# Two FNet and two MLP layers in fp32: a layer-norm shift on ScalarE, high parts first at the start, and weight steps moved in the first MLP half

## The chip, the cores and the metric

The kernel runs on 1 core of one Trainium2 chip. A core has a matrix engine (TensorE, "PE" in the profile, its weight loads "PEld"), VectorE (DVE), ScalarE (ACT), GpSimd (POOL) and SyncE (SP), which here only issues transfers. Each engine runs its own instructions in the order in which they were written; between engines they wait on semaphores. SBUF is the on-chip memory, PSUM the eight banks that matmuls write. The metric is device time in microseconds, the median of several runs.

## The reference, cut to what matters

```python
def _A_ref(x, dft_seq_re, dft_seq_im, dft_hid_re, dft_hid_im):
    a = jnp.einsum("bsd,ed->bse", x, dft_hid_re)
    b = jnp.einsum("bsd,ed->bse", x, dft_hid_im)
    return jnp.einsum("ts,bse->bte", dft_seq_re, a) - jnp.einsum("ts,bse->bte", dft_seq_im, b)

def _B_ref(x, w1, b1, w2, b2):
    y = _layernorm(x, axis=-1)
    h = _gelu(jnp.einsum("bsd,df->bsf", y, w1) + b1)
    return jnp.einsum("bsf,fd->bsd", h, w2) + b2

x = x + _A_ref(_layernorm(x), ...)     # twice this pair,
x = x + _B_ref(_layernorm(x), ...)     # with the same weights
```

x is 1 x 2048 x 576, the MLP's inner width is 4608, all in fp32. _B_ref normalises its input once more, so the kernel takes both norms in one.

## The kernel before, in words

Every matrix product is split for precision: each operand is stored as a high part (a copy in fp32r) and a low part (the operand minus the high part), and a product is three matmul passes, high x high, high x low, low x high (PASSES: which part of the left operand u, of the right operand w). ScalarE makes high parts, VectorE low parts. Most products are also cut by Strassen's scheme into seven block products per 2 x 2 blocks, numbered 1 to 7, with sums of blocks as operands.

A layer has three stages.

- Sequence transform (class Sequence). The rows of x come in eight pairs p of 128-row tiles. A pair is loaded, its mean and variance are taken (norm_stats: BN_STATS, BN_AGGR), it is normalised, and split: high_left and low_left for the block of DFT coefficients (1024 columns), high_z and low_z for the data (three blocks of 288, then one more), right_sums, high_sums and low_sums for Strassen's sums. fill() is a generator that writes these steps; run() advances it and writes first_mms(p), 48 matmuls of 288 columns for the first two output tiles, which fill all eight PSUM banks. After the eighth pair come the other 14 output tiles (mms, post), whose coefficients stream in.
- Hidden transform (function hidden), for half of the rows at a time, eight tiles n. After each tile's 54 matmuls VectorE adds the residual, and norms(n) takes the statistics, makes the normalised tile, and later PE transposes it (turn_blocks). stats() gives, in the small tile mv: mean, variance, power -1/2 of the variance, and the shift = -mean x power. normalize() is one ScalarE activation with that scale and shift. The tile n = 7 is "plain": it is normalised by VectorE and needs no shift.
- MLP (function mlp), for the same half. inner(q) makes 2 x 128 inner features: seven products in the order ORDER, each with an add on VectorE, then gelu on ScalarE. outer(g, i, side) multiplies them by w2, one Strassen product i in two product halves (jj), each 12 matmuls of 288 columns into one of two bank pairs, after which VectorE adds the bank pair into its goal (576 columns). A bank pair comes round again two product halves later. Per group g there is inner, a row of outer with four products (eight halves), inner, and a row with three products (six halves); OUTER names the products.

Only in the first MLP half of layer 1 are the weights themselves split and stored for the three later halves. weights() is a background generator for w1; pump() takes its next step, alternately VectorE's low part (384 columns) with ScalarE's next high part, and the store. make(g) does it for w2 (low parts of 2 x 288 columns on VectorE). What sets their place is written by hand: at[0] counts positions in a group, 0 to 6 the seven products of the first inner, 7 to 14 the eight halves, 15 to 21 the second inner, 22 to 27 the six halves. BEHIND lists the positions after which pump() is called; make(g) returns steps with their positions. The activation work of an inner (tasks, eight steps: gelu and high parts on ScalarE, low parts and Strassen's sums on VectorE, later ones on POOL) is taken by work(n) behind outer's halves and the next inner's products. slot[0] counts the halves of a row.

In the last group of the last half (ends), POOL adds the buffer uv, which holds product 6, to products 3, 7 and 4 before rows are stored.

Of the kernel before, what the change touches and what calls it, by code (L numbers as in the profile page):

```python
# [10 lines left out]
AF = mybir.ActivationFunctionType  # L11
# [147 lines left out]
def spectral_mixer(ctx: ExitStack, tc: tile.TileContext, x, dh, c0, cs, w1, b1, w2, b2, out):  # L159
# [58 lines left out]
    def stats(src, twice=False, plain=False):  # L218


        st, mv = (v[:, 0] for v in moments())
        st = st.rearrange("p (a b) -> p a b", a=2)
        for h in range(2):
            nc.vector.bn_stats(st[:, h, :], src[:, h, :])
        nc.vector.bn_aggr(mv[:, 0:2], st.rearrange("p a b -> p (a b)"))
        if twice:
            nc.vector.tensor_scalar(mv[:, 2:3], mv[:, 1:2], 1 + EPS, EPS * EPS, op0=OP.mult, op1=OP.add)  # L227
        else:
            nc.vector.tensor_scalar(mv[:, 2:3], mv[:, 1:2], EPS, None, op0=OP.add)
        nc.gpsimd.tensor_tensor(mv[:, 3:4], mv[:, 2:3], power[:, 0:1], op=OP.pow)  # L230
        if plain:
            return mv
        nc.gpsimd.tensor_tensor(mv[:, 4:5], mv[:, 0:1], mv[:, 3:4], op=OP.mult)
        nc.gpsimd.tensor_tensor(mv[:, 4:5], power[:, 2:3], mv[:, 4:5], op=OP.subtract)  # L234
        return mv

    def stats_of_pair(src, plain, later):

        st, mv = moments()
        for h in range(4):  # L240
            nc.vector.bn_stats(st[:, h // 2, h % 2 * 6:h % 2 * 6 + 6], src[:, h, :])
        for h in range(2):
            nc.vector.bn_aggr(mv[:, h, 0:2], st[:, h])
        (nc.gpsimd if later else nc.vector).tensor_scalar(mv[:, :, 2], mv[:, :, 1], EPS, None, op0=OP.add)
        nc.gpsimd.tensor_tensor(mv[:, :, 3], mv[:, :, 2], power[:, 0:2], op=OP.pow)
        if plain:
            return mv
        nc.gpsimd.tensor_tensor(mv[:, :, 4], mv[:, :, 0], mv[:, :, 3], op=OP.mult)
        nc.gpsimd.tensor_tensor(mv[:, :, 4], power[:, 2:4], mv[:, :, 4], op=OP.subtract)
        return mv  # L250

    def normalize(dst, src, mv):
# [72 lines left out]
    class Sequence:  # L325
        def __init__(self, src, early):

            self.src, self.early = src, early
            self.Z, self.parts, self.b12, self.v, self.x, self.mv = [None] * NP, {}, {}, {}, {}, {}
            self.ready, self.closed, self.wish = 0, False, list(range(NP))  # L330
            self.normal, self.xs, self.before = set(), [], self.prepare()
            self.pieces = self.fill()


# [31 lines left out]
        def fill(self):  # L366
# [49 lines left out]
            for p in range(NP):  # L416
# [11 lines left out]
                if p == 1 and self.early:  # L428
# [94 lines left out]
        def load_left(self, p):  # L523
            for t in range(PLAIN):
                dma(self.lv[p][:, 4 * t:4 * t + 4], c0[p][:, t])

        def norm_stats(self, p):
            if p not in self.mv:
                self.mv[p] = stats_of_pair(self.x[p], p == 0 and not self.early, p > 2)

        def normalize(self, p):
            for h in range(2):
                at = slice(2 * h, 2 * h + 2)
                if p == 0 and not self.early:
                    v, mv = self.x[p][:, at], self.mv[p][:, h]
                    nc.vector.tensor_scalar(v, v, mv[:, 0:1], mv[:, 3:4], op0=OP.subtract, op1=OP.mult)
                    continue
                normalize(self.x[p][:, at], self.x[p][:, at], self.mv[p][:, h])

        def high_left(self, p):  # L540
# [48 lines left out]
        def first_mms(self, p):  # L589
            c, z, b = self.left(p), self.Z[p](7, 2, DH), self.b12[p](2, DH)  # L590
            right = {(1, 1): z[:, 0], (2, 2): z[:, 1], (2, 1): z[:, 2], (1, 2): b}
            for t in range(PLAIN):
                for i in (1, 2):
                    for j in (1, 2):
                        o = banks[4 * (1 - t) + 2 * (i - 1) + j - 1][:, :DH]
                        for k in (1, 2):
                            for n, (u, w) in enumerate(PASSES):
                                mm(o, c[:, u, 4 * t + 2 * (i - 1) + k - 1], right[k, j][:, w],
                                   p == 0 and k == 1 and n == 0, p == NP - 1 and k == 2 and n == 2)
            self.own.give(self.parts.pop(p))  # L600
            clock[0] += 1

# [277 lines left out]
    def hidden(h, mlp):  # L880
# [18 lines left out]
        def norms(n):  # L899

            if n % 2 == 0:
                t8[n // 2] = t8s.take()
            v = t8[n // 2](8, DH)
            tile_x = xv[:, :, order[n]]

            z = v[:, 2:4] if n % 2 == 0 else v[:, 0:2]
            mv = stats(tile_x, twice=True, plain=n == NP - 1)
            yield
            if n < NP - 1:
                normalize(z, tile_x, mv)  # L910
# [160 lines left out]
    def mlp(hid, store, first, ends, before, after):  # L1071
# [40 lines left out]
        def make(g):  # L1112
# [157 lines left out]
        def outer(g, i, side):  # L1270
            for jj in range(2):
# [183 lines left out]
```

## Time and profile before

| | |
|---|---|
| median of 3 runs | 2653.71 us (2652.15 to 2653.80) |
| profiled execution | 2650.84 us |
| its span | 2649.0 us |
| TensorE clock granted | 1.00 |
| TensorE busy | 2623.9 us |
| VectorE, ScalarE, GpSimd busy | 1833.9, 1107.5, 823.3 us |

The span runs from the first to the last instruction of the profile; 1.84 us of the execution lie around it. A row of a timeline is: start, length, engine, line, operation, what it writes and reads, sizes, count, and in brackets the idle time before it and what ended it. Line L209 is mm(), L196 and L199 are add() and sub() for all engines, so rows are told apart by tiles and sizes: A and R are the two SBUF heaps (R holds split parts), bank is PSUM, moments the small tile.

The main stages in the profile: the first pairs from 8.6 to 62.5 us, the rest of the sequence transform to about 380, the hidden transform to 443, the first MLP half to 862; then hidden and MLP for the other rows, and from about 1336 the second layer.

### The profile page before, as it was taken

How to read it: one execution, taken by the hardware profiler on the slowest of the kernel's cores; microseconds unless marked ns; L12 is line 12 of the kernel's file. 1: busy time of each engine (PE TensorE's matmuls, PEld its weight loads, DVE VectorE, ACT ScalarE, POOL GpSimd, SP SyncE). 2: the span in 40 equal slices, each digit the busy share in tenths (PEclk: the TensorE clock that was granted, in tenths of full speed). 3: DMA queues.
4: the chain of work that ended last, by engine and by line, in shares of the span. 5: the costliest groups of instructions: out<-in, count | busy, mean ns of one | idle time of the engine just before them, and what ended most of it. 6: DMA issues, size and time to landing. Idle time of an engine off the chain costs nothing. (4 is left out here: it accounts for less than half of the span.)

```text
span 2649.0 us, 44753 instructions
## 1 busy us (share of the span) xinstructions
PE 2623.9 (99%) x17252; PEld 2466.2 (93%) x17252; DVE 1833.9 (69%) x2545; ACT 1107.5 (42%) x1785; POOL 823.3 (31%) x702
## 2 busy tenths in 40 slices
PE   9999999999999999999999999999999999999999
PEld 9999999888888989998999999999999999899998
DVE  8999987877777665556687777576555557655555
ACT  6555655545453343333354333353333324433332
POOL 6343434534534432222251000132222233322222
PEclk9999999999999999999999999999999999999999
DMA  5677786777778666666554333746666685666664
GB/s 183 230 271 239 245 262 209 258 268 281 270 274 282 196 193 194 199 215 207 168 199 132 123 123 123 208 144 194 196 196 195 194 271 150 204 194 195 194 196 151
DMA packets 223237, 544.90 MB, mean 206 GB/s; under 512 B 23712, under 2 KB 74912, under 8 KB 222880
## 3 DMA queue, kind: packets, MB, share of 16 engines
q1 hardware_dynamic: 209632, 511.94, 61.5%
q10 hardware_dynamic: 13392, 30.09, 2.9%
q8 instruction: 137, 2.24, 0.3%
q14 instruction: 76, 0.62, 0.1%
HBM read 429.87 MB, written 114.72 MB: 206 GB/s over the span
## 5 line engine op out<-in xcount | busy, mean ns | idle before, releaser
L209 PE MATMUL bank<-R 128*128 128x288 f32 (+2 forms) x16972 | 2592.9, 314 | 12.1 <-DVE R L199 4.4
L209 PEld LDWEIGHTS bank<-R 128*128 128x128 f32 x16972 | 2435.6, 188 | 165.3 <-DVE R L199 7.2
L196 DVE TENSOR_TENSOR A<-bank,A 128x576 f32<-128x576 f32 (+3 forms) x810 | 568.3, 708 | 529.3 <-PE bank L209 477.7
L199 POOL TENSOR_TENSOR R<-A,R 128x512 fp32r<-128x512 f32 (+1 forms) x290 | 380.8, 1321 | 901.0 <-ACT R L1245 530.4
L199 DVE TENSOR_TENSOR R<-A,R 128x1024 fp32r<-128x1024 f32 (+9 forms) x535 | 535.3, 1026 | 47.6 <-ACT R L652 13.2
L1245 ACT ACTIVATE R<-A 128x512 fp32r<-128x512 f32 x288 | 177.5, 630 | 357.3 <-DVE A L199 225.3
L196 POOL TENSOR_TENSOR A<-A 128x576 f32<-128x576 f32 (+2 forms) x102 | 151.7, 1492 | 533.4 <-ACT A L693 337.3
L1184 ACT ACTIVATE bank<-bank,b1t 128x512 f32<-128x512 f32 (+1 forms) x224 | 144.9, 647 | 369.1 <-DVE bank L196 244.0
L199 POOL TENSOR_TENSOR A<-A 128x288 f32<-128x288 f32 (+3 forms) x152 | 193.0, 1274 | 209.1 <-DVE R L199 99.6
L196 DVE TENSOR_TENSOR bank<-bank,A 128x512 f32<-128x512 f32 (+1 forms) x228 | 152.3, 670 | 144.9 <-PE bank L209 144.1
L652 ACT ACTIVATE R<-A 128x1024 fp32r<-128x1024 f32 x196 | 206.1, 1053 | 103.9 <-PE bank L209 60.4
L199 DVE TENSOR_TENSOR A<-A 128x1024 f32<-128x1024 f32 (+3 forms) x166 | 160.2, 970 | 6.2
L199 DVE TENSOR_TENSOR R<-bank,R 128x512 fp32r<-128x512 f32 x232 | 156.2, 676 | 4.3 <-ACT R L1245 3.7
L1245 ACT ACTIVATE R<-bank 128x512 fp32r<-128x512 f32 x216 | 121.2, 595 | 29.6 <-PE bank L209 29.6
L199 DVE TENSOR_TENSOR A<-bank,A 128x512 f32<-128x512 f32 x144 | 98.1, 681 | 0.1
L1211 ACT ACTIVATE A<-bank 128x512 f32<-128x512 f32 (+1 forms) x76 | 43.8, 577 | 128.8 <-PE bank L209 121.8
L279 ACT ACTIVATE R<-A 128x256 fp32r<-128x256 f32 x126 | 52.0, 413 | 64.5 <-DMA w_parts<-R 19.5
L253 ACT ACTIVATE A<-A,moments 128x576 f32<-128x576 f32 x58 | 48.6, 862 | 71.1 <-POOL moments L234 44.1
L1184 ACT ACTIVATE A<-bank,b1t 128x512 f32<-128x512 f32 (+1 forms) x76 | 50.6, 666 | 65.2 <-DVE bank L196 65.2
L230 POOL TENSOR_TENSOR moments<-moments,power 128x1 f32<-128x1 f32 x32 | 26.4, 825 | 122.2 <-DVE moments L227 122.2
L280 ACT ACTIVATE R<-A,power,middle 128x128 fp32r<-128x128 f32 x126 | 60.8, 482 | 0.0
L954 ACT ACTIVATE R<-A 128x768 fp32r<-128x768 f32 (+2 forms) x36 | 32.9, 947 | 40.1 <-DVE A L199 40.0
(64 smaller groups left out, 630.9 us busy)
## 6 DMA issues: line engine op xcount, KB each, us to landing
R<-w_parts SPq DMA_DIRECT2D x504, 320.0 KB, 3.4
R<-w_parts SPq DMA_DIRECT2D x189, 576.0 KB, 3.7
A<-in_cs SPq DMA_DIRECT2D x112, 512.0 KB, 4.4
w_parts<-R SPq DMA_DIRECT2D x63, 576.0 KB, 5.2
w_parts<-R ACTq DMA_DIRECT2D x81, 320.0 KB, 3.6
uv_mid<-A SPq DMA_DIRECT2D x28, 576.0 KB, 5.5
w_parts<-R SPq DMA_DIRECT2D x45, 320.0 KB, 3.6
A<-in_w SPq DMA_DIRECT2D x72, 192.0 KB, 5.1
```

Of the source, the lines that this page charges most:

```text
L196: engine.tensor_tensor(dst, a, b, op=op)
L199: engine.tensor_tensor(dst, a, b, op=OP.subtract)
L209: nc.tensor.matmul(o, a, b, start=start, stop=stop, skip_group_check=True)
L230: nc.gpsimd.tensor_tensor(mv[:, 3:4], mv[:, 2:3], power[:, 0:1], op=OP.pow)
L253: nc.scalar.activation(dst, src, AF.Identity, bias=mv[:, 4:5], scale=mv[:, 3:4])
L279: nc.scalar.activation(t[:, 1:4:2], src[:, 0:3:2], AF.Copy)
L280: nc.scalar.activation(t[:, 2], src[:, 1], AF.Identity, bias=power[:, 2:3], scale=middle)
L652: nc.scalar.activation(self.cells[t, i](2, NP, P)[:, 0], self.source(t, i), AF.Copy)
L954: nc.scalar.activation(y[:, i, 0:3, at], x, AF.Copy)
L1184: nc.scalar.activation(dst, src, AF.Gelu_apprx_tanh, bias=bias(f))
L1211: nc.scalar.activation(up, o, AF.Copy)
L1245: nc.scalar.activation(H[q, k](2, TC)[:, 0], src, AF.Copy)
```

## The change

It has five parts.

1. The shift. stats() no longer makes it with two POOL operations. VectorE writes -mean while POOL takes the power, and a new function shift() makes -mean x power as one ScalarE activation just before normalize(). It holds for the hidden transform's tiles 0 to 6 of all four halves and for the second pair at the start.
2. The start. The second pair's first two BN_STATS come before the first pair's low data parts, the rest right behind these, and the first pair's low left part comes after both.
3. first_mms() writes its 48 matmuls pass by pass (all high x high first) for pairs 0 to 6 of both layers; the last pair keeps the old order, cell by cell.
4. The first MLP half. The pumps at positions 7 and 23 move to 6 and 21; make()'s steps at 9, 10 and 24, 25 move to 8, 9 and 23, 24; activation steps stand behind halves 0, 1, 3, 5, 6, 7 of a row instead of 0, 1, 3, 4, 6, 7.
5. The end. POOL adds uv to products 3, 7 and 4 of the last group as soon as product 6 is there, ahead of their own VectorE adds, instead of behind these.

```diff
-BEHIND = (0, 2, 2, 4, 5, 7, 15, 17, 17, 19, 21, 23)
+BEHIND = (0, 2, 2, 4, 5, 6, 15, 17, 17, 19, 21, 21)
...
-        if plain:
-            return mv
-        nc.gpsimd.tensor_tensor(mv[:, 4:5], mv[:, 0:1], mv[:, 3:4], op=OP.mult)
-        nc.gpsimd.tensor_tensor(mv[:, 4:5], power[:, 2:3], mv[:, 4:5], op=OP.subtract)
+        if not plain:
+            nc.vector.tensor_scalar(mv[:, 4:5], mv[:, 0:1], -1.0, None, op0=OP.mult)
         return mv
...
+    def shift(mv):
+        nc.scalar.activation(mv[:, 4:5], mv[:, 4:5], AF.Identity, bias=power[:, 2:3], scale=mv[:, 3:4])
...
-                if p < 2 and not self.early:
-                    self.low_left(p)
-                    if p == 0:
-                        self.low_z(0)
-                        yield
+                if p == 0 and not self.early:
+                    self.half_stats(1)
+                    self.low_z(0)
+                    self.norm_stats(1)
+                    self.low_left(0)
+                    yield
+                if p == 1 and not self.early:
+                    self.low_left(1)
...
-            for t in range(PLAIN):
-                for i in (1, 2):
-                    for j in (1, 2):
-                        o = banks[4 * (1 - t) + 2 * (i - 1) + j - 1][:, :DH]
-                        for k in (1, 2):
-                            for n, (u, w) in enumerate(PASSES):
-                                mm(o, c[:, u, 4 * t + 2 * (i - 1) + k - 1], right[k, j][:, w],
-                                   p == 0 and k == 1 and n == 0, p == NP - 1 and k == 2 and n == 2)
+            cells = [(t, i, j, k) for t in range(PLAIN) for i in (1, 2) for j in (1, 2) for k in (1, 2)]
+            steps = [(*cell, n) for n in range(3) for cell in cells]
+            if p == NP - 1:
+                steps = [(*cell, n) for cell in cells for n in range(3)]
+            for t, i, j, k, n in steps:
+                o, (u, w) = banks[4 * (1 - t) + 2 * (i - 1) + j - 1][:, :DH], PASSES[n]
+                mm(o, c[:, u, 4 * t + 2 * (i - 1) + k - 1], right[k, j][:, w],
+                   p == 0 and k == 1 and n == 0, p == NP - 1 and k == 2 and n == 2)
...
-            return (list(zip((24, 25), one)),
-                    list(zip((0, 1, 2, 3, 9, 10, 15, 16, 17, 18, 19, 20), five + six + three + seven + four + two)))
+            return (list(zip((23, 24), one)),
+                    list(zip((0, 1, 2, 3, 8, 9, 15, 16, 17, 18, 19, 20), five + six + three + seven + four + two)))
...
-                if g == last and (i in (3, 7) or i == 4 and not ends):
+                if g == last and i in (3, 7, 4) and not ends:
                     add(nc.gpsimd, to, to, uv[:, 2 * jj:2 * jj + 2])
                 if g == last:
-                    if ends and i == 3:
-                        to = goal[4][:, 2 * jj:2 * jj + 2]
-                        add(nc.gpsimd, to, to, uv[:, 2 * jj:2 * jj + 2])
+                    if ends and i == 6:
+                        for k, m in ((3, 1), (7, 0), (7, 1), (4, 0), (4, 1)) if jj else ((3, 0),):
+                            to = goal[k][:, 2 * m:2 * m + 2]
+                            add(nc.gpsimd, to, to, uv[:, 2 * m:2 * m + 2])
...
-                work(1 + (slot[0] == 0) if g == last - 1 and side == 0 else slot[0] % 3 < 2)
+                work(1 + (slot[0] == 0) if g == last - 1 and side == 0 else slot[0] in (0, 1, 3, 5, 6, 7) if first else slot[0] % 3 < 2)
```

Three places in the order of instructions. First VectorE at the start, before: behind the first pair's normalising (128x576) stand the left part (1024), the data parts (3x288, 288), and then the second pair's measuring.

```order
L536 TENSOR_SCALAR A<-A,moments 128x576 x2
L199 TENSOR_TENSOR R<-A,R 128x1024
L199 TENSOR_TENSOR R<-A,R 128x3x288
L199 TENSOR_TENSOR R<-A,R 128x288
L241 BN_STATS moments<-A 128x6 x4
L243 BN_AGGR moments<-moments 128x2 x2
L244 TENSOR_SCALAR moments<-moments 128x2
```

And now:

```order
L549 TENSOR_SCALAR A<-A,moments 128x576 x2
L240 BN_STATS moments<-A 128x6 x2
L199 TENSOR_TENSOR R<-A,R 128x3x288
L199 TENSOR_TENSOR R<-A,R 128x288
L240 BN_STATS moments<-A 128x6 x2
L245 BN_AGGR moments<-moments 128x2 x2
L246 TENSOR_SCALAR moments<-moments 128x2
L249 TENSOR_SCALAR moments<-moments 128x2
L199 TENSOR_TENSOR R<-A,R 128x1024
```

Half of the measuring moved ahead of the data parts, the left part behind all of it, and one small step (L249) is new.

Second, ScalarE at two tiles of the hidden transform, before: each normalising (L253) reads a shift that POOL has made.

```order
L202 ACTIVATE R<-A 128x1152
L253 ACTIVATE A<-A,moments 128x576
L927 ACTIVATE A<-A 128x384
L945 ACTIVATE A<-bank 128x4x256
L946 ACTIVATE A<-bank 96x4x128
```

And now, with the shift (L236) on ScalarE itself:

```order
L202 ACTIVATE R<-A 128x1152
L236 ACTIVATE moments<-moments,power 128x1
L256 ACTIVATE A<-A,moments 128x576
L943 ACTIVATE A<-A 128x384
L961 ACTIVATE A<-bank 128x4x256
L962 ACTIVATE A<-bank 96x4x128
```

One instruction came in front of each normalising; on POOL two went from behind each power.

Third, VectorE in a row of six halves in the first MLP half, before: bank<-bank ends the inner, 128x576 is the add behind a half, the pairs with 128x512 are activation steps, 3x128 is a weight step of w1, 2x288 one of w2.

```order
L196 TENSOR_TENSOR bank<-bank,A 128x512
L196 TENSOR_TENSOR A<-bank,A 128x576 x2
L199 TENSOR_TENSOR R<-bank,R 128x512
L196 TENSOR_TENSOR A<-bank,A 128x512
L199 TENSOR_TENSOR R<-A,R 128x3x128
L196 TENSOR_TENSOR A<-bank,A 128x576 x2
L199 TENSOR_TENSOR R<-bank,R 128x512
L199 TENSOR_TENSOR A<-bank,A 128x512
L199 TENSOR_TENSOR R<-A,R 128x2x288
L196 TENSOR_TENSOR A<-bank,A 128x576
L199 TENSOR_TENSOR R<-bank,R 128x512
L199 TENSOR_TENSOR A<-A,bank 128x512
```

And now:

```order
L196 TENSOR_TENSOR bank<-bank,A 128x512
L199 TENSOR_TENSOR R<-A,R 128x3x128
L196 TENSOR_TENSOR A<-bank,A 128x576 x2
L199 TENSOR_TENSOR R<-bank,R 128x512
L196 TENSOR_TENSOR A<-bank,A 128x512
L196 TENSOR_TENSOR A<-bank,A 128x576
L199 TENSOR_TENSOR R<-A,R 128x2x288
L196 TENSOR_TENSOR A<-bank,A 128x576
L199 TENSOR_TENSOR R<-bank,R 128x512
L199 TENSOR_TENSOR A<-bank,A 128x512
L196 TENSOR_TENSOR A<-bank,A 128x576 x2
```

The w1 step moved ahead of the first add, the w2 step behind the third, which carries no activation step, and the third activation step from the fifth half to the sixth.

More of the change, by code (lines that the diff above doesn't have):

```diff
@@ L230, in stats, with measure, stats_of_pair @@
         nc.gpsimd.tensor_tensor(mv[:, 3:4], mv[:, 2:3], power[:, 0:1], op=OP.pow)
[L231 to L240 removed]
+        if not plain:
+            nc.vector.tensor_scalar(mv[:, 4:5], mv[:, 0:1], -1.0, None, op0=OP.mult)
+        return mv
+    def shift(mv):
+        nc.scalar.activation(mv[:, 4:5], mv[:, 4:5], AF.Identity, bias=power[:, 2:3], scale=mv[:, 3:4])
+    def measure(src, st, halves):
+        for h in halves:
             nc.vector.bn_stats(st[:, h // 2, h % 2 * 6:h % 2 * 6 + 6], src[:, h, :])
+    def stats_of_pair(st, mv, plain, later, quick):
         for h in range(2):
@@ L245, in stats_of_pair @@
         nc.gpsimd.tensor_tensor(mv[:, :, 3], mv[:, :, 2], power[:, 0:2], op=OP.pow)
[L246 to L249, printed above, removed]
+        if quick:
+            nc.vector.tensor_scalar(mv[:, :, 4], mv[:, :, 0], -1.0, None, op0=OP.mult)
+        elif not plain:
+            nc.gpsimd.tensor_tensor(mv[:, :, 4], mv[:, :, 0], mv[:, :, 3], op=OP.mult)
+            nc.gpsimd.tensor_tensor(mv[:, :, 4], power[:, 2:4], mv[:, :, 4], op=OP.subtract)
         return mv
@@ L330, in __init__ @@
             self.ready, self.closed, self.wish = 0, False, list(range(NP))
[L331 removed]
+            self.normal, self.begun, self.xs, self.before = set(), {}, [], self.prepare()
             self.pieces = self.fill()
@@ L525, in load_left, with half_stats @@
                 dma(self.lv[p][:, 4 * t:4 * t + 4], c0[p][:, t])
+        def half_stats(self, p):
+            self.begun[p] = moments()
+            measure(self.x[p], self.begun[p][0], range(2))
         def norm_stats(self, p):
             if p not in self.mv:
-                self.mv[p] = stats_of_pair(self.x[p], p == 0 and not self.early, p > 2)
+                halves = range(2 if p in self.begun else 0, 4)
+                st, mv = self.begun.pop(p, None) or moments()
+                measure(self.x[p], st, halves)
+                self.mv[p] = stats_of_pair(st, mv, p == 0 and not self.early, p > 2, p == 1 and not self.early)
         def normalize(self, p):
@@ L537, in normalize @@
                     continue
+                if p == 1 and not self.early:
+                    shift(self.mv[p][:, h])
                 normalize(self.x[p][:, at], self.x[p][:, at], self.mv[p][:, h])
@@ L909, in norms @@
             if n < NP - 1:
+                shift(mv)
                 normalize(z, tile_x, mv)
```

## The prediction

> **What bounds the kernel now.** I read the page's first part, then the matrix engine's own waits, longest in total first.
>
> ```profile
> PE 2623.9 (99%) x17252; PEld 2466.2 (93%) x17252; DVE 1833.9 (69%) x2545; ACT 1107.5 (42%) x1785; POOL 823.3 (31%) x702
> PE bank L941 <- ACT A L253: 5.6, 8, 0.8
> PE bank L209 <- DVE R L199: 4.4, 8, 1.0
> PE bank L209 <- DVE A L196: 3.1, 8, 0.8
> ```
>
> TensorE is busy 99% of the span, and no matmul is removed. A gain can only be time in which TensorE waits. The page hides part of that: the modelled end of a pipelined matmul covers the start of each wait. So I look for places where the same work takes longer. Four matter: the normalised tiles (first wait above), the start (second), the first MLP half (third) and the stores at the end.
>
> **The normalised tiles.** Rows of the timeline: a tile whose transposes wait, and one (401.60) whose do not.
>
> ```profile
> 401.60 1.04 PE L941 MATMUL bank<-ident,A 128*128 128x128 f32 x8
> ...
> 414.18 1.05 POOL L230 TENSOR_TENSOR moments<-moments,power 128x1 f32<-128x1 f32 x1 [6.20 <-DVE moments L227]
> 415.30 0.81 POOL L233 TENSOR_TENSOR moments<-moments 128x1 f32<-128x1 f32 x1
> 416.18 1.18 POOL L234 TENSOR_TENSOR moments<-power,moments 128x1 f32<-128x1 f32 x1
> 417.29 0.38 PE L941 MATMUL bank<-ident,A 128*128 128x128 f32 x2
> 417.40 0.87 ACT L253 ACTIVATE A<-A,moments 128x576 f32<-128x576 f32 x1 [2.68 <-POOL moments L234]
> 418.32 0.88 PE L941 MATMUL bank<-ident,A 128*128 128x128 f32 x6 [0.65 <-ACT A L253]
> ```
>
> The chain is power (POOL), product (POOL), difference (POOL), normalising activation (ACT), transposes (PE). The eight transposes take 1.04 us in one piece; here 418.32 + 0.88 - 417.29 = 1.91, so the wait costs 0.87 us where 0.65 is shown idle. There are 8 such waits, so up to 7.0 us.
>
> The change removes the two POOL operations after the power. A VectorE step of one number per row makes the negated mean beside the power, and ACT makes the shift as its own instruction.
>
> ```profile
> 2.01 0.20 ACT L1378 ACTIVATE power<-middle 128x4 f32<-128x4 f32 x1
> ```
>
> That is the nearest row for the new ACT instruction: 0.20 us. The far bound is the 0.87 of the wide activation. The power ends at 415.23; shift and normalising end at 416.30 with 0.20 and 416.97 with 0.87. The third transpose is due about 417.5, so both bounds lie under PE's earlier work and the wait goes altogether. Behind the shift on ACT's queue stands only what stood behind the normalising before, and that now starts earlier. The VectorE step delays the DVE queue by less than the 0.20, where nothing is late. I take 7.0 us; the low end is the shown idle alone, 5.6. Late next is the last tile's chain, which the change leaves and which starts from PE itself.
>
> **The first MLP half.** Four such halves run, with the same matmuls each; here the first two, by windows, then the one window that I need for a rival.
>
> ```profile
> 443.29:830.87 387.58, 382.63 (x2225) 1.00 0.76 262
> 927.27:1304.58 377.31, 376.46 (x2225) 1.00 0.65 198
> 402.90:417.00 14.10, 14.10 (x108) 1.00 0.66 189
> ```
>
> The first half takes 10.3 us more. Only in it does VectorE also make weights. The extra is a pattern that repeats per group; one row of ACT's timeline, VectorE's, then PE's:
>
> ```profile
> 507.94 0.66 ACT L1184 ACTIVATE bank<-bank,b1t 128x512 f32<-128x512 f32 x1 [0.93 <-DVE bank L196]
> ...
> 511.10 0.68 DVE L199 TENSOR_TENSOR R<-bank,R 128x512 fp32r<-128x512 f32 x1
> 511.70 0.68 DVE L196 TENSOR_TENSOR A<-bank,A 128x512 f32<-128x512 f32 x1
> 512.30 0.55 DVE L199 TENSOR_TENSOR R<-A,R 128x384 fp32r<-128x384 f32 x1
> 512.76 1.59 DVE L196 TENSOR_TENSOR A<-bank,A 128x576 f32<-128x576 f32 x2
> ...
> 536.80 0.75 DVE L199 TENSOR_TENSOR R<-A,R 128x576 fp32r<-128x576 f32 x1
> 537.47 0.75 DVE L196 TENSOR_TENSOR A<-bank,A 128x576 f32<-128x576 f32 x1
> ...
> 538.37 3.88 PE L209 MATMUL bank<-R 128*128 128x288 f32 x25 [0.30 <-DVE A L196]
> ...
> 462.68 0.50 PE L209 MATMUL bank<-R 128*128 128x512 f32 x1 [0.47 <-ACT A L1211]
> 469.95 0.50 PE L209 MATMUL bank<-R 128*128 128x512 f32 x1 [0.47 <-DVE bank L196]
> 802.98 0.50 PE L209 MATMUL bank<-R 128*128 128x512 f32 x1 [0.79 <-DVE A L196]
> ```
>
> A product half is 12 matmuls of 288 columns, 1.6 us at 132 ns each (402.90 row: 14.10 us for 108 gives 131). VectorE must then add it (576, 0.67 from start to start). An activation step behind it is two operations of 512, 1.2 us (511.10 to 512.30). A weight operation adds 0.46 (384: 512.30 to 512.76) or 0.67 (576: 536.80 to 537.47). Add, step and 576 together are 2.5 us against 1.6, and the next add comes late; two halves on, PE wants the bank.
>
> The change takes the weight operation away at both places. At 536.80 it goes one product half ahead, behind a half with no step: the add that ran at 537.47 could run at 536.80 and end at 537.55. PE wanted it at about 538.37 - 0.30 - 0.22 = 537.85 (0.22 is the hidden part found above), so 0.3 us is spare. The activation step that followed at the next half moves one half on, so two heavy halves no longer adjoin. At 512.30 the 384 goes ahead of the first add, where VectorE waits for PE anyway: the adds run from 512.30, 0.46 earlier. On ACT the two copies that start the next weight block go with it, ahead of the step's gelu at 507.94. They are narrower than its 512 columns, so under 1.3 us together, of which the 0.93 idle before it hides most; VectorE needs the step's result only after its second add, at 511.10. The transfers issued two positions behind a weight step move with it on SP's queue by one half; their order on it stays, and what they load is wanted several products later.
>
> Not touched are the waits at 462.68, 469.95 and 802.98: 1.73 us idle, plus 0.22 and a slow restart each, about 2.5 us. So 10.3 - 2.5 = 7.8 us goes. Ends: 3.9, if the waits come back at every second place, and 8.5, as other halves wait a little too. Late next is the wait at 802.98.
>
> **The start.** Timeline rows, all four engines; the last three are of the end of the same stage.
>
> ```profile
> 7.74 2.56 DVE L199 TENSOR_TENSOR R<-A,R 128x1024 fp32r<-128x1024 f32 x3 [0.27 <-ACT R L542]
> 8.57 0.40 PE L209 MATMUL bank<-R 128*128 128x288 f32 x1
> 9.98 6.51 PE L209 MATMUL bank<-R 128*128 128x288 f32 x47 [1.01 <-DVE R L199]
> 12.27 1.14 POOL L245 TENSOR_TENSOR moments<-moments,power 128x2 f32<-128x2 f32 x1 [5.92 <-DVE moments L244]
> 14.35 1.63 ACT L253 ACTIVATE A<-A,moments 128x576 f32<-128x576 f32 x2 [3.91 <-POOL moments L249]
> 16.97 2.74 DVE L199 TENSOR_TENSOR R<-A,R 128x864 fp32r<-128x864 f32 x3 [0.98 <-ACT R L554]
> 18.09 12.20 PE L209 MATMUL bank<-R 128*128 128x288 f32 x90 [0.70 <-DVE R L199]
> ...
> 54.84 3.89 DVE L199 TENSOR_TENSOR R<-A,R 128x864 fp32r<-128x864 f32 x4 [1.58 <-ACT R L554]
> ...
> 66.98 2.49 DVE L199 TENSOR_TENSOR R<-A,R 128x1152 fp32r<-128x1152 f32 x2 [1.90 <-ACT R L583]
> 69.53 0.67 PE L209 MATMUL bank<-R 128*128 128x288 f32 x3 [0.24 <-DVE R L199]
> ```
>
> From 8.57 to 18.09 PE does 49 matmuls that need 6.5 us: 3.0 are lost. With the high-times-high pass first, PE has 16 matmuls (2.1 us) before it needs a low part and 16 more before a low left part, so the wait at 9.98 goes. The second pair's measuring comes ahead of the first left subtraction (about 1.1 us of the 2.56), and its shift no longer passes POOL twice (14.35 minus the power's end at 13.41), so its values are ready some 1.5 us earlier.
>
> But not all of that stays. From 16.97 VectorE runs this stage without a pause, at PE's own pace, and the last pair keeps the old order, which needs its low parts in the second matmul. So what counts is how much earlier VectorE gets going. It loses 0.98 us before 16.97, waiting for the values that now come early; the new step costs it up to 0.2. I take 0.8: the whole chain through 54.84 and 66.98 to the wait at 69.53 moves by that. Ends: 0, if the second pair's data, now read earlier, is late on a queue that is loading all inputs; 3.0, if all is kept.
>
> **The end.**
>
> ```profile
> 2634.16 8.36 POOL L196 TENSOR_TENSOR A<-A 128x576 f32<-128x576 f32 x6 [10.48 <-DVE A L196]
> 2644.43 0.46 DVE L196 TENSOR_TENSOR A<-bank,A 128x288 f32<-128x288 f32 x1 [0.26 <-PE bank L209]
> DMA to landing us min/median/max: 1.9/2.9/5.2
> ```
>
> Stores of two products wait for these six POOL adds until 2642.5 and crowd in front of the last store. The adds now run two products earlier, and each store leaves after its own VectorE add. From 2644.89 to the span's end are 4.1 us. If the last store lands in 1.9, 2.2 are gained; if it is as before, none. I take 1.0, about the median less the minimum.
>
> **The sum.** 7.0 + 7.8 + 0.8 + 1.0 = 16.6 us. The profiled execution took 2650.84 us (span 2649.0 and 1.84 around it), so 2634.2. The runs' median, 2653.71, lies 2.87 above the profiled one; kept, that gives 2637.1.
>
> **Rivals.**
>
> The MLP waits come back. Three activation steps in a row now stand behind the last three halves of the longer row, with 0.3 us spare each. If a weight step runs longer than 0.75, half of the term is lost: 16.6 - 3.9 = 12.7, so 2641.0. Against it: the two banked steps read PSUM and took 0.68 at every place above. Chance 0.17.
>
> The change does not do what it says on POOL: the power, 1.05 us, could stretch until the shift comes no earlier. Then 9.6 remain, 2644.1. Nothing but the two removed operations lies between, so 0.07, with late data at the start as a part of it.
>
> Slower: the new pass order steps through all eight banks, two matmuls each, where the old one stayed six on a bank. If that slows a matmul, 2 layers x 7 pairs x 48 = 672 of them pay. It decides at 16.6 us / 672 = 25 ns each; at twice the 132 ns it would cost 88.7 and give 2725.8. Against it: the rows at 402.90 alternate between two banks at every matmul, at 131 ns and granted clock 1.00. Chance 0.02. The Trainium skill, "TensorE: Matmul & The Clock Gate", section "A second HAM failure mode: psum-queue depth-cycling", speaks for it: cycling through PSUM banks let TensorE idle briefly between groups and its clock swing between half and full. By that rule the result is the 2725.8; the clock in the row above does not bear it out.
>
> **How the numbers follow.** My forecast, a gain of 13 to 19.5 us, has 0.66. More has 0.03. The MLP rival 0.17, the POOL and data cases 0.07, no change (several of these together) 0.04, slower 0.03, most of it the banks. A measurement of this kernel tells about 0.2% (5.3 us) from nothing; faster than that has 0.93, within 0.04, slower 0.03. The range runs from all terms at their better ends but not all at once (2634.0) through the MLP rival to the first of the POOL cases (2643.5).
>
> **What would show it.** Right: no wait of L941 on ACT; the first MLP half within 3 us of the second; the matmul spacing still 132 ns; the wait at 69.53 still there, about 0.8 us earlier; no six POOL adds after 2634. Wrong: VectorE waiting on a transfer before its first measuring; waits on the adds between 500 and 830 us; a clock under 1.00 in the input stage.

## The result, and the profile after

| | before | after |
|---|---|---|
| median | 2653.76 us (2651.19 to 2654.54, 6 runs) | 2633.61 us (2632.50 to 2634.11, 6 runs) |
| profiled execution | 2650.84 us | 2634.11 us |
| its span | 2649.0 us | 2632.3 us |

The ratio is 0.9926, with a 95% interval of 0.9916 to 0.9937: 20.15 us, or 0.74%, faster. The two profiled executions differ by 16.7 us. Why the two differences are not the same is one of the questions below. Medians below leave out three executions that took more than 4000 us at a lower granted clock (one of the kernel before, one with the shift alone, one with the pumps alone).

From the page and from the matrix engine's waits of the changed kernel:

```profile
PE 2617.2 (99%) x17252; PEld 2466.4 (94%) x17252; DVE 1834.1 (70%) x2574; ACT 1118.3 (42%) x1815; POOL 796.7 (30%) x644
PE bank L209 <- DVE R L199: 3.8, 8, 1.2
PE bank L209 <- ACT R L569: 1.2, 1, 1.2
PE bank L209 <- DVE A L196: 0.5, 1, 0.5
```

The waits of the transposes on ScalarE (L941 before, L957 now) are gone from the list. Of the eight on VectorE's adds one is left. The one on the second pair's high parts (L569 now, L554 before) grew from 0.5 to 1.2 us.

Timeline rows at the tile that the prediction showed, POOL, ScalarE, TensorE:

```profile
414.03 0.55 POOL L230 TENSOR_TENSOR moments<-moments,power 128x1 f32<-128x1 f32 x1 [6.20 <-DVE moments L232]
414.61 0.39 ACT L236 ACTIVATE moments<-moments,power 128x1 f32<-128x1 f32 x1
415.03 0.87 ACT L256 ACTIVATE A<-A,moments 128x576 f32<-128x576 f32 x1
417.14 1.04 PE L957 MATMUL bank<-ident,A 128*128 128x128 f32 x8
```

Power, shift and normalising now follow each other with only the power on POOL, and the eight transposes run in one piece of 1.04 us. The shift on ScalarE took 0.39 us, inside the bounds of 0.20 and 0.87. The normalised tile is ready 1.2 us before the transposes start. The power took 0.55 us here, and 1.04 at the next tile that waited before (429.86), whose transposes run in one piece too.

TensorE's stages by windows (start and end, length, busy time, matmuls, granted clock, DMA share, GB/s): first MLP half, second MLP half, the second hidden half, and six pairs of layer 2's first stage:

```profile
441.33:819.73 378.40, 376.60 (x2225) 1.00 0.78 268
914.24:1291.61 377.37, 376.54 (x2225) 1.00 0.65 198
819.73:914.24 94.51, 93.96 (x711) 1.00 0.79 250
1324.17:1362.26 38.09, 38.09 (x291) 1.00 0.80 284
```

The first MLP half is 9.2 us shorter than before (387.58) and 1.0 longer than the second. The last window runs from the start of one pair's matmuls to that of the sixth pair after it, 6 x 48 in the new pass order (its count includes three neighbours): 38.09 us, 132 ns each, at clock 1.00; in the old order these matmuls took 38.08 us. Stepping through the banks costs nothing here.

VectorE's rows at the place of the prediction's 511.10 and 512.30:

```profile
506.23 0.55 DVE L199 TENSOR_TENSOR R<-A,R 128x384 fp32r<-128x384 f32 x1
507.23 0.76 DVE L196 TENSOR_TENSOR A<-bank,A 128x576 f32<-128x576 f32 x1 [0.45 <-PE bank L209]
508.84 0.76 DVE L196 TENSOR_TENSOR A<-bank,A 128x576 f32<-128x576 f32 x1 [0.86 <-PE bank L209]
...
510.11 1.34 DVE L196 TENSOR_TENSOR A<-bank,A 128x512 f32<-128x512 f32 x2
511.38 0.75 DVE L199 TENSOR_TENSOR R<-A,R 128x576 fp32r<-128x576 f32 x1
```

The 384 step now fills time in which VectorE would wait for TensorE (0.45 us is left of it). The row of 1.34 us is the second operation of an activation step and, right behind it, the next add.

The start and the end:

```profile
8.93 6.68 PE L209 MATMUL bank<-R 128*128 128x288 f32 x48
16.79 4.45 PE L209 MATMUL bank<-R 128*128 128x288 f32 x31 [1.18 <-ACT R L569]
55.76 13.23 PE L209 MATMUL bank<-R 128*128 128x288 f32 x97 [0.42 <-DVE R L199]
69.33 1.88 PE L209 MATMUL bank<-R 128*128 128x288 f32 x12 [0.34 <-DVE R L199]
...
2617.19 6.97 POOL L196 TENSOR_TENSOR A<-A 128x576 f32<-128x576 f32 x5 [0.16 <-DVE A L196]
2629.05 0.46 DVE L196 TENSOR_TENSOR A<-bank,A 128x288 f32<-128x288 f32 x1 [0.26 <-PE bank L209]
```

The first pair's 48 matmuls run without a stop. A wait for the second pair's high parts follows, another comes at the last pair (55.76), and the one at 69.53 stays, 0.2 us earlier. POOL's adds are over at 2624.2, and from the last VectorE add (2629.51) to the end of the span are 2.8 us, where it was 4.1.

### The profile page after: what moved, and what is told of

The parts are those of the page before. It is cut to its first block, busy times and chain, and to the rows that moved or that the text cites. A ratio compares the mean times of both kernels' runs of the same rounds, so it can differ in the third digit from the quotient of the medians.

```text
span 2632.3 us, 44772 instructions
## 1 busy us (share of the span) xinstructions
PE 2617.2 (99%) x17252; PEld 2466.4 (94%) x17252; DVE 1834.1 (70%) x2574; ACT 1118.3 (42%) x1815; POOL 796.7 (30%) x644
## 5 line engine op out<-in xcount | busy, mean ns | idle before, releaser
L1135 ACT ACTIVATE R<-A 128x576 fp32r<-128x576 f32 x63 | 42.2, 676 | 15.8 <-DVE A L199 7.2
```

The costliest lines, as they stand in the source:

```text
L1135: nc.scalar.activation(got2[g, i](2, 2, DH)[:, :, 0], src, AF.Copy)
```

## The parts one by one

**The shift alone**

```diff
-        nc.gpsimd.tensor_tensor(mv[:, 4:5], mv[:, 0:1], mv[:, 3:4], op=OP.mult)
-        nc.gpsimd.tensor_tensor(mv[:, 4:5], power[:, 2:3], mv[:, 4:5], op=OP.subtract)
+            nc.vector.tensor_scalar(mv[:, 4:5], mv[:, 0:1], -1.0, None, op0=OP.mult)
...
+                shift(mv)
```

> Only the shift of the hidden transform's tiles is on ScalarE (part 1 without the second pair). Theory A, each part removes its own TensorE waits and the gains add: the eight L941 waits on ACT go, 0.87 us each as the pieces of the transposes show, the four hidden halves together are 6.9 us shorter, and the median falls by 6.9 us; layer 2's first pairs are as before. Rival B, the normalising was only the last of several late things: the waits go but half of the time returns at another wait of the same half, so under 4 us. For the new waits in layer 2's first pairs of the changed kernel (1.2 us): if the shift made them they are here, if they come from a coefficient block that happened to land late they come or go in any kernel.

Measured: 2645.36 us against 2652.77 us before, ratio 0.9970 (0.9958 to 0.9982), so 7.4 us. The second hidden half by windows of TensorE, before and with the shift alone:

```profile
830.87:927.27 96.40, 94.39 (x710) 1.00 0.77 245
...
831.69:926.19 94.50, 93.95 (x711) 1.00 0.78 250
```

1.90 us for two tiles, as in the changed kernel (94.51). Theory A holds.

**The MLP part alone**

```diff
-BEHIND = (0, 2, 2, 4, 5, 7, 15, 17, 17, 19, 21, 23)
+BEHIND = (0, 2, 2, 4, 5, 6, 15, 17, 17, 19, 21, 21)
...
-            return (list(zip((24, 25), one)),
+            return (list(zip((23, 24), one)),
...
-... zip((0, 1, 2, 3, 9, 10, 15, ...
+... zip((0, 1, 2, 3, 8, 9, 15, ...
...
-                work(... slot[0] % 3 < 2)
+                work(... slot[0] in (0, 1, 3, 5, 6, 7) if first else slot[0] % 3 < 2)
```

> Only part 4, the moved weight and activation steps of the first MLP half. Theory A: the first half falls from 387.6 to 378.4 us, all else as before, so the median falls by 9.2 us, and the wait at 802.98 goes as it did in the changed kernel. Rival B, part of the 9.2 us needs the earlier arrival of another part: then 7.8 us as forecast, with the wait at 802.98 still there. Layer 2 has the code of before here: new waits of about 1.2 us in its first pairs would then be chance of a transfer.

Measured: 2641.85 us, ratio 0.9958 (0.9946 to 0.9971), 10.9 us; the interval runs from 7.7 to 14.3. The first MLP half:

```profile
443.67:821.89 378.22, 376.52 (x2226) 1.00 0.78 268
```

9.4 us shorter, and the wait at 802.98 is gone without any other part. Rival B falls.

**The start alone**

```diff
+                    self.half_stats(1)
+                    self.low_z(0)
+                    self.norm_stats(1)
+                    self.low_left(0)
...
+            steps = [(*cell, n) for n in range(3) for cell in cells]
```

> Only parts 2 and 3, with the second pair's shift on ScalarE: the start's order, and the pass order for pairs 0 to 6 of both layers. Theory A: 0.4 to 0.8 us less, all of it in layer 1's first pairs (53.9 to 53.2 us); layer 2's first stage within 0.3 us of before. Rival B, the pass order makes layer 2's VectorE chain late at the last pair: layer 2's sequence transform is 1.2 us longer, so the whole gains nothing or loses up to 0.8 us. Rival C, stepping through all banks slows matmuls: spacing over 132 ns and slower by 16 us or more.

Measured: 2652.21 us, ratio 0.9996 (0.9987 to 1.0005): no difference that can be told. The first pairs took 53.2 us, as A said. Layer 2's first pairs were 0.8 us longer, with a wait at the last pair, where B put it; the section on layer 2 below shows that the pass order alone does not make it.

**The end alone**

```diff
-                    if ends and i == 3:
-                        to = goal[4][:, 2 * jj:2 * jj + 2]
+                    if ends and i == 6:
+                        for k, m in ((3, 1), (7, 0), (7, 1), (4, 0), (4, 1)) if jj else ((3, 0),):
```

> Only part 5, POOL's adds of product 6 at the end. Theory A: the stretch from the last matmul to the end of the span falls from 4.9 to 3.6 us, so 1.3 us less. Rival B: the earlier adds slow VectorE's own adds of products 3 and 7, TensorE waits for a bank pair in the last four products and at least half of the 1.3 us returns there. Layer 2's first pairs have the code of before: its waits show what chance does.

Measured: 2651.56 us, ratio 0.9994 (0.9985 to 1.0003). From the last matmul's start to the end of the span the trace has 3.6 us instead of 4.9, and the stretch of the last products is as long as before (32.2 us), so A, though so little can't be told in the times.

The differences of the four medians add up to 7.4 + 10.9 + 0.6 + 1.2 = 20.1 us, the whole change to 20.15. Each of the four is known to a few us only, so that the sum comes this close is partly luck.

## Which edit does it in the MLP half

**The pumps alone** (BEHIND as above)

> Of part 4 only the pumps (positions 7 and 23 to 6 and 21). Theory A, the three edits of part 4 remove different waits: in the kernel before, a wait of 0.25 us in the row of six (first at 513.66) follows VectorE's 384 step, and one of 0.46 in the row of eight (first at 538.37) follows its 576 step. Then the seven waits of the first kind go, with 0.11 us of slow restart each: 2.5 us less, the first half 385.1 us, and the 0.46 waits stay. Rival B, it needs all three edits at once: no more than 1 us. Open is which edit took the wait at 802.98: if the pumps, 1.0 us more.

Measured: 2653.05 against 2652.64 us, ratio 1.0003 (0.9993 to 1.0012). The half took 388.24 us, 0.7 longer than before. Windows, then VectorE's and TensorE's rows:

```profile
444.39:832.63 388.24, 382.08 (x2225) 1.00 0.76 261
...
516.82 0.75 DVE L199 TENSOR_TENSOR R<-A,R 128x576 fp32r<-128x576 f32 x1
517.48 0.75 DVE L196 TENSOR_TENSOR A<-bank,A 128x576 f32<-128x576 f32 x1
...
518.29 0.96 PE L209 MATMUL bank<-R 128*128 128x512 f32 x3 [0.21 <-DVE A L196]
```

The wait at the 384 step is gone, but a little later an add stands behind the 576 step, and TensorE stops there instead: a wait moved. So much for this edit is as rival B said; that it takes all three edits is not so (below).

**make()'s steps alone** (positions 8, 9 and 23, 24)

> Of part 4 only make()'s steps (9, 10 and 24, 25 to 8, 9 and 23, 24). Theory A: the seven 0.46 us waits of the row of eight and what follows them (0.11 to 0.22) go, 4.0 to 4.7 us less; the 0.25 us waits of the row of six stay or grow, because the 576 step now follows the 384 step more closely there. So the first half at 383 to 384 us. Rival B: the wait only moves one product half on, and less than 1 us is gained.

Measured: 2645.74 us, ratio 0.9976 (0.9966 to 0.9985), 6.9 us.

```profile
443.11:825.21 382.10, 379.78 (x2225) 1.00 0.77 266
```

5.5 us less, more than A's 4.7, because this edit also takes the wait at 802.98. VectorE and POOL there, before and then with make()'s steps alone:

```profile
797.96 4.36 DVE L199 TENSOR_TENSOR R<-A,R 128x576 fp32r<-128x576 f32 x3
...
793.08 2.96 POOL L199 TENSOR_TENSOR A<-A 128x576 f32<-128x576 f32 x2 [9.90 <-DVE R L199]
796.00 5.91 POOL L199 TENSOR_TENSOR R<-A,R 128x512 fp32r<-128x512 f32 x4
```

```profile
793.89 3.41 DVE L199 TENSOR_TENSOR R<-A,R 128x576 fp32r<-128x576 f32 x3
...
787.15 2.95 POOL L199 TENSOR_TENSOR A<-A 128x576 f32<-128x576 f32 x2 [7.87 <-DVE R L199]
790.05 2.55 POOL L199 TENSOR_TENSOR R<-A,R 128x512 fp32r<-128x512 f32 x2
793.37 3.05 POOL L199 TENSOR_TENSOR R<-A,R 128x512 fp32r<-128x512 f32 x2 [0.77 <-ACT R L1245]
```

make()'s step brings two sums on POOL with it (x2 at 793.08). Before, these were late, POOL's four low parts ran without a pause until 801.91, and VectorE's three weight steps beside them took 4.36 us; they take 3.41 with the sums one product half earlier. Taken one by one, the last of the three, a 384 step, took 1.65 us before and 0.55 now, when POOL had already stopped at 796.42. The add that TensorE waits for came that much later. The Trainium skill, "SBUF — State Buffer", section "Who interferes with whom", says that a VectorE instruction with two SBUF inputs contends with a GpSimd instruction that reads SBUF. The rows agree: a 384 step also takes 0.55 us at 506.23 above, where POOL is idle. No run moves the sums alone, so this cause is read from the rows.

**The activation steps alone** (halves 0, 1, 3, 5, 6, 7)

> Of part 4 only the activation steps (behind halves 0, 1, 3, 5, 6, 7). Theory A: the add that is late at 537.47 stands behind a half with both an activation step and the 576 step, and this edit leaves it there, so the 0.46 us waits stay; only the small second wait behind them goes: 0 to 1.5 us less. Rival B: it is two heavy halves side by side that make the wait; then this edit alone takes the 0.46 us waits, 4 us or more.

Measured: 2650.78 us, ratio 0.9992 (0.9983 to 1.0001). The half took 386.40 us, 1.2 less. A holds for the half; in the times it can't be told.

**Pumps and make()'s steps together**

> Of part 4 the pumps and make()'s steps together, the activation steps as before. Alone the pumps made the first half 0.7 us longer (388.2 us), make()'s steps 5.5 shorter (382.1), the activation steps 1.2 shorter (386.4); all three together 9.4 (378.2). Theory A: pumps and make()'s steps need each other, since behind the pumps alone VectorE's 576 step, and behind make()'s steps alone its 384 step, still makes an add late; with both gone there is nothing left for the activation steps to take, and the half takes 378.2 to 378.6 us. Rival B, the three edits work on different waits: the activation steps' 1.2 us is still missing, 379.4 us or more.

Measured: 2642.97 us, ratio 0.9965 (0.9951 to 0.9979).

```profile
443.95:822.57 378.62, 376.88 (x2225) 1.00 0.78 268
```

9.0 us less, at the edge of A's figure. One by one the edits gave -0.7, 5.5 and 1.2 us, these two together 9.0: either alone leaves one weight step behind which an add is late. The pumps' move is worth something only beside make()'s steps, there 3.5 us; these help alone too. The activation steps add at most 0.4 us, so the prediction's reason that two heavy halves no longer adjoin is worth little.

**A wait that is left.** The changed kernel with the last group's w2 steps moved too:

```diff
-                return (list(zip((22, 23, 26), one + five[:1])),
+                return (list(zip((22, 25, 27), one + five[:1])),
```

> The changed kernel with one more move: the last group's w2 steps in its row of six at positions 22, 25, 27 instead of 22, 23, 26. Theory A: the wait of 0.70 us at 827.06 (on VectorE's add, which stands behind this 576 step and two activation steps) goes, and the first half is 377.6 us instead of 378.4; in time 0.8 us less than the changed kernel, which its measurement can hardly tell. Rival B: ScalarE's next high part, now two positions later, or the sums on POOL make the next products late, and a wait of the same size comes in the row of eight or the last products.

Measured: 2634.32 us, 0.9932 (0.9917 to 0.9946) of before, against 0.9926 for the changed kernel: no difference. The wait at 827.06 lies behind the half's last 512-column matmul, so in the next window, and that one took 94.32 us instead of 94.51. The starts of the matmuls show that 0.7 us went at 827, and 0.3 came back four us later. The trace names no releaser there; by the times it is ScalarE's high part of an activation step, which ends at 830.54, when TensorE goes on. Rival B, in part; that the wait counts in this window I had overlooked.

## The start, taken apart

**The pass order alone**

> Part 3 alone, the pass order of first_mms. Theory A: the wait of 1.28 us at 9.98 goes (TensorE has 16 matmuls before it needs a low part), but the second pair's values come no earlier, so the next wait (1.62 us in two pieces at 16.99 and 18.09) grows by what was gained; layer 1's first pairs take 53.9 us as before, within 0.3. Rival B: the gain stays, and they take 53.2 as in the changed kernel; then the order of VectorE's steps does nothing. Matmul spacing 132 ns by both.

Measured: 2653.00 against 2652.93 us, ratio 0.9999 (0.9990 to 1.0009). TensorE's rows:

```profile
9.06 6.68 PE L209 MATMUL bank<-R 128*128 128x288 f32 x48
17.47 7.73 PE L209 MATMUL bank<-R 128*128 128x288 f32 x56 [1.74 <-ACT R L554]
```

The first 48 run in one piece, and all of it is given back at the second pair. The first pairs take 53.7 us. A holds.

**VectorE's order alone**

> Part 2 alone with the second pair's shift, the old order of matmuls. Theory A: VectorE gets going earlier in the second pair, but TensorE needs the first pair's low left part at its third matmul and that now comes behind the second pair's measuring, so the wait near 10 us grows by 1 to 2 us and the one near 17 shrinks; what counts at the end of the stage is VectorE's chain, 53.2 to 53.9 us. Rival B: the longer first wait stays, because PE is then behind for good: 54.5 us or more.

Measured: 2653.08 us, ratio 0.9999 (0.9989 to 1.0008). TensorE's rows, then windows: the first pairs, a stretch of them, and all up to the first MLP half; the last line is the latter in the kernel before.

```profile
9.66 0.40 PE L209 MATMUL bank<-R 128*128 128x288 f32 x1 [0.60 <-DVE R L199]
12.40 12.78 PE L209 MATMUL bank<-R 128*128 128x288 f32 x74 [2.34 <-DVE R L199]
...
8.69:65.76 57.07, 54.13 (x388) 0.94 0.48 171
12.40:20.00 7.60, 7.60 (x36) 0.60 1.06 392
8.69:444.06 435.37, 429.75 (x3208) 0.99 0.70 235
```

```profile
8.57:443.29 434.72, 427.97 (x3205) 1.00 0.71 236
```

The first pairs took 3.1 us longer, as B said and more, because behind the pause the clock fell to 0.60. Yet at the first MLP half only 0.7 us of it is left: the waits at 69.5, 82.8, 90.6 and 114.7 of the kernel before became shorter or went. In this execution TensorE found again most of what it had lost in its first 60 us. That is A's mechanism, in a later stage than A put it. Whether a gain there is lost in the same way is not shown: counted from the first matmul, 1.1 us were still there at the hidden transform with the start alone, and 0.5 in the changed kernel. The two halves of the start need each other, but together they move little.

## Where layer 2 lost a microsecond

Layer 2's first pairs took 50.8 us before and 51.3 after, with new waits of TensorE there. ScalarE's row at the second block of coefficients, before and after, then with the shift alone and with the MLP part alone (both have the code of before here):

```profile
1321.89 1.06 ACT L542 ACTIVATE R<-A 128x1024 fp32r<-128x1024 f32 x1 [6.90 <-DMA A<-in_c]
```

```profile
1310.66 1.06 ACT L557 ACTIVATE R<-A 128x1024 fp32r<-128x1024 f32 x1 [8.63 <-DMA A<-in_c]
```

```profile
1322.39 1.06 ACT L543 ACTIVATE R<-A 128x1024 fp32r<-128x1024 f32 x1 [8.44 <-DMA A<-in_c]
```

```profile
1313.16 1.06 ACT L542 ACTIVATE R<-A 128x1024 fp32r<-128x1024 f32 x1 [7.14 <-DMA A<-in_c]
```

In the profiles of the 14 kernels this transfer took 2.9 to 4.0 us in seven and 4.25 to 4.9 in the other seven. In the first seven the first pairs took 50.8 to 51.1 us, in the others 51.3 to 52.7. Both kinds of code are in both groups. The wait that follows comes some 40 to 60 us after the block, at the fifth pair with the old order of matmuls, and at the last pair, which keeps that order, with the new one. TensorE's rows, first with the shift alone, then in the changed kernel:

```profile
1363.19 7.05 PE L209 MATMUL bank<-R 128*128 128x288 f32 x51 [0.69 <-DVE R L199]
```

```profile
1369.15 6.12 PE L209 MATMUL bank<-R 128*128 128x288 f32 x44 [0.25 <-DVE R L199]
```

With the shift on POOL (next section), which has the new order, the block was early and there is no such wait. So the new code alone does not make it: it goes with when a block lands in that execution. Whether the new order makes a late block likelier is open; four of the five kernels that have it were late, and three of the nine others.

## Is ScalarE needed for the shift?

The changed kernel, with VectorE's negated mean multiplied by the power on POOL, one operation instead of the two of before:

```diff
             nc.vector.tensor_scalar(mv[:, 4:5], mv[:, 0:1], -1.0, None, op0=OP.mult)
+            nc.gpsimd.tensor_tensor(mv[:, 4:5], mv[:, 4:5], mv[:, 3:4], op=OP.mult)
...
-                shift(mv)
```

> The changed kernel, but the hidden tiles' shift is one POOL product of VectorE's negated mean and the power, and not a ScalarE step. Theory A, what mattered was to shorten POOL's three steps, and there is room to spare: power, one product (0.55 to 1.2 us each) and the normalising end before the third transpose is due, so the eight L941 waits stay away and the hidden halves are as in the changed kernel (94.5 and 93.8 us), within 0.3. Rival B, ScalarE's shift is needed: a wait of 0.3 us or more comes back at each of the eight tiles, 2.4 us or more in all.

Measured: 2639.71 us, 0.9947 (0.9933 to 0.9962) of before; the changed kernel has 0.9926 (0.9916 to 0.9937). The two intervals overlap a little, so the traces have to tell. The second hidden half by windows, then ScalarE, POOL, VectorE and TensorE in the first:

```profile
820.94:916.33 95.39, 94.21 (x710) 1.00 0.77 248
...
422.34 0.87 ACT L257 ACTIVATE A<-A,moments 128x576 f32<-128x576 f32 x1 [1.48 <-POOL moments L233]
421.25 1.05 POOL L233 TENSOR_TENSOR moments<-moments 128x1 f32<-128x1 f32 x1
423.98 2.46 DVE L199 TENSOR_TENSOR R<-A,R 32x256 fp32r<-32x256 f32 x4 [1.72 <-ACT R L970]
435.50 2.25 PE L209 MATMUL bank<-R 128*128 128x288 f32 x15 [0.63 <-DVE R L199]
```

The transposes don't wait, so far A. But beside VectorE's steps the product took 1.05 us, ScalarE stood still for 1.48, the high parts behind the normalising on its queue came late, VectorE waited 1.72 for them, and its low parts came too late for TensorE. The wait is back under another name: 0.9 us in each of the four hidden halves, 3.5 in all, and 0.2 to 0.3 more at the start of each MLP half. B's price, at another place than B put it.

## Why the prediction was right, and where not

The sum was made against one execution: 2634.2 us forecast, 2634.11 in the profiled one of the changed kernel. That match is partly luck, as the terms show. By medians the gain is 20.15 us (16.7 to 22.3 by the interval), just past the 19.5 at which the forecast ended, and 2633.61 lies 0.4 us under the range's lower end of 2634.0. By stages:

| term | forecast | traces | that part alone, medians |
|---|---|---|---|
| normalised tiles | 7.0 | 7.4 | 7.4 |
| first MLP half | 7.8 | 9.2 | 10.9 |
| the start | 0.8 | 0.8 in the first pairs | 0.6 |
| the end | 1.0 | 1.3 | 1.2 |

Unrounded, the traces' terms come to 18.5 us, where the spans differ by 16.7. Lost on the way are 0.4 us by which the first matmul came later, 1.2 in and around layer 2's first pairs, and 0.2 in the rest of layer 1's sequence transform. The forecast had no such losses and smaller terms; the two errors cancel.

- The tiles: right in step, and nearly in size. Eight waits went, by the transposes' starts 0.87 to 0.97 us each, 0.93 on average; the forecast took the smallest, 0.87, for all, and rightly not the 0.65 that the wait shows.
- The first MLP half: right in mechanism, mis-sized. The step that failed is "Not touched are the waits at 462.68, 469.95 and 802.98". The third was touched: by the matmuls' starts it cost 0.96 us, and 0.11 is left. I followed make()'s step on VectorE, ScalarE and SP, and left out the two sums that it issues on POOL. The subtraction also took the second half as free of waits, but it has 0.5 us of its own. 7.8 + 0.9 + 0.5 is the 9.2. "Late next is the wait at 802.98" was wrong with it; late next is the one at 827.06.
- The start: the size in its own stage came out, the account did not. The first matmul came 0.4 us later (in the 14 kernels it starts anywhere from 8.57 to 9.93), and the waits just ahead of and at 69.33 are 0.2 longer, so the wait at 69.53 moved by 0.2, not 0.8. The waits at 16.79 (1.34 us by the starts) and 55.76 (0.58), which keep the gain small, were not foreseen. What the 0.8 us is worth at the end is not settled: among the seven kernels with the old start and the old tiles, the time from the first matmul to the first MLP half varies from 433.7 to 436.3 us.
- The end: 1.3 us instead of 1.0. The last store now takes 2.8 us from its add, not the 1.9 of the quickest.
- The offset: "kept, that gives 2637.1" failed. The profiled execution of before lies below all six of its runs, that of the changed kernel is the highest of its six. That is nearly all of the 3.5 us between forecast and median. The one of before is an execution in which the first matmul and layer 2's block came early.
- The rivals. The MLP waits did not come back with the whole change; the pumps alone show what that rival would have looked like. The data at the start was late by a little: VectorE's first measuring of the second pair (7.67) waited 0.17 us for its transfer, a sign that the prediction had named as wrong; its next step then waited 0.43 for ScalarE anyway. POOL did not stretch the power, but the one POOL product shows what a longer chain there costs. The pass order cost nothing: 132 ns per matmul at clock 1.00. The Trainium skill's rule on cycling through PSUM banks ("TensorE: Matmul & The Clock Gate", "A second HAM failure mode: psum-queue depth-cycling") doesn't bear here; TensorE has no gap between those matmuls.

## What to carry to other kernels

When an engine paces another by a ring of buffers, count what stands ahead of each hand-over, on every engine that the moved step feeds: here the pumps' move, which takes one late add away, is worth nothing until the other one goes too. Compare stages by the starts of their matmuls, not by the list of waits: with make()'s steps alone the list names no wait on an add, and the half is still 3.9 us longer than with the whole part. And a forecast made against one execution needs to know where that one lies among the others before an offset is added to it.

## What the runs showed of the hardware

- In two executions TensorE's clock fell behind short pauses early in the program. With VectorE's order alone it stood 0.60 and 2.34 us within 3.4, and then ran 24 matmuls at 240 ns each; the window from 12.40 to 20.00 has clock 0.60. With the end alone, whose start is that of before, pauses of 0.49 and 1.02 us were followed, eight matmuls on, by 13 at 240 ns:

```profile
12.00:16.00 4.00, 4.00 (x21) 0.60 1.06 395
```

  In the kernel before a pause of 1.02 us at 10, and with the pass order alone one of 1.74 us at 17, left it at 1.00. The Trainium skill ("TensorE: Matmul & The Clock Gate", "HAM oscillation — how this bites in real kernels") puts the limit at idle gaps of about 3.4 us; in these two executions no pause was longer than 2.34. No run changes the pauses alone, so that they are the cause is argued.
- One product of one number per row took 0.19 us on POOL at one tile (431.61 in the kernel with the shift on POOL), and 1.05 at the tile before (421.25), where it ended together with a 1152-wide step of VectorE.
- One transfer, issued at the same point, takes 2.9 to 4.9 us, and with the longer ones go waits of up to 2 us on TensorE some 40 to 60 us later.
